# Four masked tiles to one crossbar transpose: a threshold attention with a two-layer block behind it

## The chip, the cores and the metric

The kernel runs on one core of a Trainium2 chip. The metric is the device time of one execution in microseconds (us). Before the change three timed runs gave 505.51, 511.03 and 508.68 us; the median is 508.68.

The names used below are those of the profile. PE is the matrix engine, PEld its loading of weights. DVE, ACT and POOL are the vector, scalar and general engines, and SP is an engine that only issues DMAs here. "SPq" and "ACTq" are the queues of SP and ACT, where DMAs are issued.

## The reference: what is computed

For 8 batches and 8 heads, with 576 rows of 64 elements, the attention keeps only the scores that come within tau = 0.02 of their row's largest one. The result, put together as 4608 rows of 512, goes through a block of two layers (512 to 2048 to 512) whose nonlinearity is h - tanh(h).

```python
scores = scale * np.matmul(q, k.transpose(0, 1, 3, 2))
thresh = np.max(scores, axis=-1, keepdims=True) - tau
scores = np.where(scores >= thresh, scores, -1000000000.0)
attn = np.exp(scores - np.max(scores, axis=-1, keepdims=True))
attn = attn / (np.sum(attn, axis=-1, keepdims=True) + 1e-09)
x = np.matmul(attn, v)            # then (batch, row, head * 64)
h = x @ w_in
out = (h - np.tanh(h)) @ w_out
```

## The kernel before

**Tiles.** Two heads make a pair; there are 32 pairs. A pair has 1152 query rows, which are nine tiles of 128 rows, so there are 288 tiles, numbered i. Each tile has 576 scores per row. Even tiles are of kind A and odd ones of kind B, and an A with the B behind it is a couple: most of the work on weights is done by couples.

**One tile's way.** `scores(i)` (L387) lets PE make the scores from the halves of q and k, of which k is there in a second form with its halves swapped (kS); DVE copies them out of the accumulator, scaled, into a buffer `sc` and finds the row's maximum (L420). `shift(i)` (L426) makes the bias tau minus maximum for a couple on DVE (L432). `kink(i)` (L439) is the mask: one ACT instruction (L447) turns each score below the threshold into a huge negative number and writes a half of the couple's buffer `z`, 128 x 576 in bf16. Then z has to be transposed, in nine blocks of 128 columns for a couple. In the first six pairs (54 tiles, `on_pe`, L57) PE does so (L466) and ACT takes the exponential from its accumulator (L475). From pair 6 on a crossbar transpose does it, a DMA that SP issues once for each couple (L454), 117 in all; its result is the buffer `zT`. `weights(i)` (L456) lets ACT take the exponential of the nine blocks in one instruction (L483, result `pT`), and `attend(i)` (L488) multiplies them with v on PE (L506, L513, L524). `norm` divides by the sum on DVE, and `emit_x` (L551) transposes the result on PE into the input of the layers.

**Other transposes.** From pair 8 or 9 on, q and k are also transposed by the crossbar (L315, 24 and 23 transposes), from the same SP queue. SP also issues the loads of the weights (L739, L743), the loads of q, k and v of the first pairs, and the stores of the output (L620, L626). Later loads of q, k and v are issued by ACT (L175).

**Layers.** The two layers work on blocks of 512 rows, made by four pairs. For each block there are 16 hidden steps, h (`hidden`, L575: four matmuls, L579; then tanh on ACT, L592, and a product on DVE, L598), and 16 projection steps, y (`project`, L603: four matmuls each, L605). They are spread over the slots of the attention by hand, as strings: one sign for a slot, h or y for a step.

**Order.** The program is written out by hand, and each engine takes its instructions in that order. The loop at L852 runs over slots s from -8 on. In slot s stand: the scores of tile s + AHEAD (8 slots ahead of the tile's own slot), the masks of tile s + MASK (5 ahead), the tanh of hidden steps written in an earlier slot, the weights of the tile whose turn it is, the layer steps of the slot, DVE's product, and the attention of the tile LAG = 2 slots behind its weights. `SOONER` (L844) takes the weights of the first four pairs four slots ahead. The loads, splits and transposes of q, k and v stand in a table of distances to the pair's first scores (L747 to L817), so they move with AHEAD.

**Buffers.** A buffer of a pool is given out again in turn, and its next writer waits until its last reader is done: for z in the crossbar part the reader is the transpose, which is done when it has landed. `z` has 4 buffers of two tiles each, `zT` 6, `sc` AHEAD - MASK + 2 = 5. So a couple's first mask waits for the transpose of the couple four before.

The lines around the change:

Of the kernel before, what the change touches and what calls it, by code (L numbers as in the profile page):

```python
# [10 lines left out]
BF16 = mybir.dt.bfloat16  # L11
# [3 lines left out]
ACT = mybir.ActivationFunctionType  # L15
# [3 lines left out]
def kernel(  # L19
# [11 lines left out]
    nc = tc.nc  # L31
    P = 128

    B, H, S, D = q.shape
# [9 lines left out]
    STEEP = 1.0e30  # L44

    HPAIR = H // 2
# [5 lines left out]
    TPP = 9  # L52
    NTILE = NPAIR * TPP
# [3 lines left out]
    def on_pe(i):  # L57
        p, j = divmod(i, TPP)
        return p < 6

    W = 2 * S

    AHEAD = 8
    LDK = 16
    MASK = 5
    LAG = 2


# [30 lines left out]
    for i in range(6):  # L99
# [8 lines left out]
    pool = lambda name, bufs, **kw: ctx.enter_context(  # L108
        tc.tile_pool(name=name, bufs=bufs, **kw)
    )  # L110
# [3 lines left out]
    qk_pool = pool("qk", 3)  # L114
    sc_pool = pool("sc", AHEAD - MASK + 2)
    st_pool = pool("st", 12)
    z_pool = pool("z", 4)
    zt_pool = pool("zt", 6)
    p_pool = pool("p", 3)
    o_pool = pool("o", 2)  # L120
    wt_pool = pool("wt", 4)
# [177 lines left out]
    def k_lead(p):  # L299
        if p < HPAIR + 2:  # L300
            return 6 if p in (2, 4) or p == HPAIR + 1 else 5 - (p == 1)
        return (6, 6)[1 - p % 2]

    def q_by_dma(p):

        return p >= DUAL
# [33 lines left out]
    def turn_first(t, part):  # L340

        hl = hls[0, t[0]]
        c0, c1 = ((0, 5), (5, TPP))[part]
        pl, tag = (ps_y, "y") if t == "ks" else (ps_h, "h")
        ps = pl.tile([P, 5 * P], FP16, name=f"ps1_{t}", tag=tag)
        for c in range(c0, c1):
            o = ps[:, (c - c0) * P : (c - c0 + 1) * P]
            if t == "ks":
                for a in range(2):
                    turn_chunk(o[64 * a : 64 * a + 64, :], c, hl[:, c, 1 - a, :])  # L350
            else:
                turn_chunk(o, c, hl[:, c, :, :].rearrange("p a d -> p (a d)"))
        if part == 0:
            mats[0, t] = qk_tile(t)
        dst, n = mats[0, t][:, c0 * P : c1 * P], (c1 - c0) * P
        if part == 1 or t == "q":
            nc.scalar.copy(out=dst, in_=ps[:, 0:n])
        else:
            nc.vector.tensor_copy(out=dst, in_=ps[:, 0:n])
# [15 lines left out]
    scs, mxs, nbs, zs, zts, pts, ops = {}, {}, {}, {}, {}, {}, {}  # L375

    def kind(i):

        return "AB"[i % 2]

    def place(i):

        p, j = divmod(i, TPP)
        j = j - p % 2
        return (p, None, 4) if j in (-1, 8) else (p, j // 4, j % 4)
# [40 lines left out]
    def shift(i):  # L426

        if kind(i) == "A":
            return
        mx = mxs.pop(i)  # L430
        nb = st_pool.tile([P, 9], F32, name="nb", tag="nb")
        nc.vector.tensor_scalar(  # L432
            out=nb.rearrange("p (a b) -> p a b", b=3)[:, :, 0:2],
            in0=mx.rearrange("p (a b) -> p a b", b=4)[:, :, 0:3],
            scalar1=-1.0, scalar2=tau, op0=ALU.mult, op1=ALU.add,
        )
        nbs[i - 1], nbs[i] = nb[:, 0:1], nb[:, 1:2]

    def kink(i):  # L439
        sc, nb = scs.pop(i), nbs.pop(i)  # L440
        if kind(i) == "B":
            zt = zs.pop(i - 1)
            z = zt[:, S:W]
        else:
            zt = zs[i] = z_pool.tile([P, W], BF16, name="z")
            z = zt[:, 0:S]
        nc.scalar.activation(  # L447
            out=z, in_=sc, func=ACT.Prelu, bias=nb, scale=1.0, alpha=STEEP
        )
        if on_pe(i):  # L450
            zts[i] = zt
        elif kind(i) == "B":
            zts[i] = zt_pool.tile([P, TPP, P], BF16, name="zT")
            nc.sync.dma_start_transpose(out=zts[i], in_=zt)  # L454

    def weights(i):  # L456

# [130 lines left out]
    def bend():  # L588
        while halves:
            m, n, ps = halves.pop(0)  # L590
            th = t_pool.tile([P, MB], F32, name="th", tag="th")
            nc.scalar.activation(out=th, in_=ps, func=ACT.Tanh)  # L592
            ths.append((m, n, ps, th))

    def shrink():
        while ths:
            m, n, ps, th = ths.pop(0)
            nc.vector.scalar_tensor_tensor(  # L598
                out=gs[m][:, n, :], in0=th, scalar=-1.0, in1=ps,
                op0=ALU.mult, op1=ALU.add,  # L600
            )

    def project(m, ms, part, ps, last, cols=slice(0, d_model)):  # L603
# [26 lines left out]
                    )  # L630


    EARLY = lambda m: 3 if m else 3
    LAST = 1

    PATTERN = lambda m: {
        0: '-h--h-hh--h-hh-h-hh-h--hh-h--hh-y-yy',
        B - 2: 'hyhyhyhyhyhyhyhyhyhyhyhyhyhyhyhy',
    }.get(m, 'h-yhyhhyhyyhyyhh-yhhyhhy-yhyyh-yyhhy')

# [3 lines left out]
    def layers(m, tail, pattern=None):  # L644
# [27 lines left out]

        now = quarters(m - 1)[EARLY(m - 1) :] if m > 0 else []
        if m < NMB - 1:
            now += quarters(m)[: EARLY(m)]
        else:
# [3 lines left out]

        ahead = n - max(0, EARLY(m) - 3) - LAST if m < NMB - 1 else n - 9 - LAST
        steps, at, i = [], [], 0
# [46 lines left out]
    def w_cast():  # L729
        flat, wt, i, cols = loaded.pop(0)  # L730
        nc.gpsimd.tensor_copy(out=flat[:, i * cols : (i + 1) * cols], in_=wt)
# [52 lines left out]
    for p in range(DUAL, NPAIR):  # L784
        first = TPP * p - AHEAD
        at = lambda d, f: plan.setdefault(first - d, []).append(f)
# [11 lines left out]
    for p in range(1, DUAL):  # L798
        first = TPP * p - AHEAD
        for d, f in PREP[3 if p == 1 else 0 :]:  # L800
            d -= p == 1 and d == 3
            if p > HPAIR and d >= LDK - 2:
                d = ((16, 14, 12), (17, 15, 13))[1 - p % 2][LDK - d]
            elif d in (7, 8) and q_by_dma(p):
                d = ((9, 9) if d == 7 else (10, 10))[1 - p % 2]
            elif p in LEADS and d in (8, 7, 5, 4):
                d = LEADS[p][(8, 7, 5, 4).index(d)]
            elif d == 4:
                d = 4
            elif d == 5:  # L810
                d = k_lead(p)
            elif p in (2, 4):
                d = {8: 9, 7: 8}.get(d, d)
            plan.setdefault(first - d, []).append(lambda p=p, f=f: f(p))
        d = (6, 7)[1 - p % 2] if q_by_dma(p) else 3 - (p == 1 or p >= 5)
        d = LEADS[p][4] if p in LEADS else d
# [21 lines left out]
    for at in sorted(plan):  # L838
        if at < -AHEAD:
            plan.setdefault(-AHEAD, []).extend(plan.pop(at))  # L840

    SOONER = (4, 4, 4, 4, 0, 0, 0)  # L844
    kinks, wts, atts = {}, {}, {}
    for i in range(NTILE + 3):
        at = i - SOONER[min(i // TPP, 6)]
        atts.setdefault(at + LAG, []).append(i)
        if i < NTILE:
            wts.setdefault(at, []).append(i)  # L850
            kinks.setdefault(i // 2 * 2 + 2 - AHEAD if i < 4 else i - MASK, []).append(i)
    for s in range(-AHEAD, NTILE + LAG + 3):  # L852
        p, j = divmod(max(s, 0), TPP)
        if 0 <= s < NTILE and j == 2 + LAG and p % HPAIR == 0 and p >= HPAIR:
            assert not todo
            todo = [(s + i, step) for i, step in layers(stage, False, PATTERN(stage))]
            stage += 1
        if s == NTILE:
            todo = [(s + n, step) for n, step in enumerate(layers(stage, True))]
            stage += 1  # L860
        if 0 <= s + AHEAD - 1 < NTILE:
            shift(s + AHEAD - 1)

        n = s + AHEAD
        if 0 < n < NTILE and place(n)[1] is None and kind(n) == "B":
            scores(n - 1)
        if 0 <= n < NTILE and (place(n)[1] is not None or kind(n) == "B"):
            scores(n)
        if s == 1 - AHEAD:
            for t in ("k", "q", "ks"):  # L870
                turn_first(t, 1)
        for i in kinks.pop(s, []):
            kink(i)
        bend()
        for i in wts.pop(s, []):
            weights(i)
        while todo and todo[0][0] <= s < NTILE + FIRST:
            todo.pop(0)[1]()
        if s == 0:
            nc.vector.tensor_tensor(  # L880
                out=fold, in0=ident_bf[:, 0:64], in1=ident_bf[:, 64:P], op=ALU.add
            )
        shrink()
        for store in going:
            store()
        going = stores[:-1]
        del stores[:-1]
        for i in atts.pop(s, []):
            pp, jj = divmod(i, TPP)
            if i < NTILE:  # L890
                attend(i)
                odd = pp % 2
                if jj == 3 + odd:
                    norm(pp, 0)
                elif odd and jj in (0, 8):
                    norm(pp - (jj == 0), 1)
            if pp and jj == 1 + pp % 2:
                emit_x(pp - 1)
        for step in plan.pop(s, []):
            step()  # L900
        for _ in range(cast_when.count(s + AHEAD)):
            w_cast()
        for _ in range(load_when.count(s + AHEAD)):
            w_load(next(pieces))
# [56 lines left out]
```

## Time and profile before

| | |
|---|---|
| timed runs, us | 505.51, 511.03, 508.68 (median 508.68) |
| span of the profiled execution, us | 509.7 |
| mean granted clock of PE | 0.997 |
| PE busy, us | 484.8 |
| ACT busy, us | 431.7 |
| DVE busy, us | 400.2 |
| POOL busy, us | 291.4 |
| mask L447 on ACT | 288 x 770 ns |
| exponential L483 on ACT | 117 x 1155 ns |
| tanh L592 on ACT | 128 x 583 ns |
| transposes zT on SP | 117, issue 1.47 us in the median |
| the same, from issue to landing, us | 3.2 least, 4.7 median, 9.8 most |

The span reaches from the first to the last instruction of one execution, which the hardware profiler recorded. An engine's busy time is the time in which its instructions were in work; overlapping instructions count once. Issuing a DMA and waiting count as no work. Matmuls are pipelined and their ends are modelled, so a busy PE need not be one at its peak. An idle time is put down to the event that ended it, for instance "ACT pT L483 <- DMA zT<-z": ACT's instruction in line 483 began when a transpose had landed.

### The profile page before, as it was taken

Reading aid. Unit: us, or ns where it says so; the run is one execution under the profiler, and the core shown is the slowest. Engines: PE = TensorE matmul, PEld = TensorE weight load, DVE = VectorE, ACT = ScalarE, POOL = GpSimd, SP = SyncE. Lnnn points to the kernel's source line nnn. Section 1 sums busy time; section 2 is a strip of 40 time slices with the busy share of each in tenths; the row PEclk is TensorE's granted clock in tenths of the full one; section 3 lists DMA queues with packets and bytes.
Section 4 is the critical chain, followed back from the end, with each engine's and each line's share of the span. In section 5 each row is a group of like instructions: output and inputs, shape, how many; then the busy total and the mean of one; then the engine's idle time right before and its main releaser. Section 6 shows DMA issues by size and latency. Waiting matters only on the chain.

```text
span 509.7 us, 12184 instructions
## 1 busy us (share of the span) xinstructions
PE 484.8 (95%) x4283; PEld 270.9 (53%) x4345; DVE 400.2 (79%) x1150; ACT 431.7 (85%) x617; POOL 291.4 (57%) x390
## 2 busy tenths in 40 slices
PE   8999899889999989999999999999998999999997
PEld 4666566445555545555555555555554555544444
DVE  5899978878889879988898789889886887544440
ACT  5999998889999889999999999899979999533430
POOL 8999999886765375757675666569456700000000
PEclk9999999989999999999999999999999999999999
DMA  7852658999999999999999999999999986311013
GB/s 206 262 155 89 195 190 220 159 225 214 231 217 245 192 254 209 238 241 242 242 195 221 261 238 225 207 242 240 213 191 258 187 144 115 87 41 42 23 41 82
DMA packets 233341, 95.32 MB, mean 187 GB/s; under 512 B 203968, under 2 KB 222656, under 8 KB 233280
## 3 DMA queue, kind: packets, MB, share of 16 engines
q1 hardware_dynamic: 212336, 72.87, 75.1%
q10 hardware_dynamic: 20944, 21.67, 16.1%
q8 instruction: 34, 0.56, 0.5%
q14 instruction: 27, 0.22, 0.2%
HBM read 36.70 MB, written 9.44 MB: 91 GB/s over the span
## 4 chain that ended last, share of the span: by engine, by line
PE 57%; POOL 12%; DMA 9%; issue 7%; ACT 7%; DVE 5%; ACTq 1%; SPq 0%; POOLq 0%; DVEq 0%
PE psY L605 18%; PE psH L579 14%; PE psS L410 13%; DMA zT<-z 6%; PE psO L513 3%; POOL kS L337 3%; PE psHt L579 3%; ACT pT L483 3%; DMA vraw<-in_v_dram 3%; ACT z L447 2%; DVE g L598 2%; POOL qhl L232 2%; DVE sc L420 2%; PE psS L401 2%; ACTq L175 1%
## 5 line engine op out<-in xcount | busy, mean ns | idle before, releaser
L420 DVE TENSOR_SCALAR_CACHE_REDUCE sc<-psS 128x576 f32<-128x576 f32 x288 | 213.5, 752 | 27.1 <-PE psS L410 12.9
L447 ACT ACTIVATE z<-sc,nb 128x576 bf16<-128x576 f32 x288 | 216.1, 770 | 8.0 <-DVE nb L432 5.7
L483 ACT ACTIVATE pT<-zT 128x1152 f16<-128x1152 bf16 x117 | 135.2, 1155 | 12.3 <-DMA zT<-z 10.6
L605 PE MATMUL psY<-w_out_sb,g 128*128 128x512 bf16 (+1 forms) x564 | 140.8, 373 | 1.6 <-issue 0.2
L579 PE MATMUL psH<-xT,w_in_sb 128*128 128x512 bf16 x448 | 119.4, 381 | 5.1 <-issue 2.0
L337 POOL COPY kS<-kT 64x1152 f16<-64x1152 f16 x62 | 70.8, 1142 | 86.3 <-DMA kT<-khl 72.7
L598 DVE SCALAR_TENSOR_TENSOR g<-th,psH 128x512 bf16<-128x512 f32 x128 | 87.6, 685 | 33.6 <-ACT th L592 32.9
L410 PE MATMUL psS<-kT,qT 128*128 128x512 f16 (+1 forms) x512 | 104.7, 286 | 4.1 <-DVE sc L420 1.9
L410 PE MATMUL psS<-kS,qT 128*128 128x512 f16 (+1 forms) x512 | 105.1, 287 | 0.0
L410 PEld LDWEIGHTS <-qT 128*128 128x128 f16 x1024 | 72.5, 98 | 59.0 <-issue 3.8
L592 ACT ACTIVATE th<-psH 128x512 f32<-128x512 f32 x128 | 74.6, 583 | 21.4 <-PE psH L579 21.4
L605 PEld LDWEIGHTS <-g 128*128 128x128 bf16 x592 | 51.1, 98 | 54.6 <-DVE g L598 0.4
L579 PEld LDWEIGHTS <-w_in_sb 128*128 128x128 bf16 x576 | 49.4, 98 | 57.4 <-issue 6.3
L513 PE MATMUL psO<-vb,pT 128*128 128x65 bf16 x1024 | 53.3, 194 | 0.0
L513 PEld LDWEIGHTS <-pT 128*128 128x128 f16 x1024 | 44.2, 98 | 9.6
L232 POOL TENSOR_TENSOR qhl<-qraw,qhl 128x576 f16<-128x576 f32 x31 | 39.7, 1281 | 2.6
L232 POOL TENSOR_TENSOR khl<-kraw,khl 128x576 f16<-128x576 f32 x31 | 39.7, 1280 | 2.7
L475 ACT ACTIVATE pT<-psZ 128x512 f16<-128x512 bf16 (+1 forms) x54 | 35.1, 654 | 2.4 <-PE psZ L466 2.1
L506 PE MATMUL psO<-vb,pT 128*128 128x130 bf16 x128 | 28.2, 220 | 3.7 <-ACT pT L483 3.6
L617 DVE COPY yo<-psY 128x512 f32<-128x512 f32 (+1 forms) x31 | 21.1, 680 | 13.1 <-PE psY L605 12.4
L539 DVE TENSOR_TENSOR osb<-psO,rc 128x256 bf16<-128x256 f32 x64 | 27.2, 424 | 2.2
L228 POOL TENSOR_SCALAR qraw<-qraw 128x576 f32<-128x576 f32 x31 | 20.8, 671 | 11.1 <-DMA qraw<-in_q_dram 10.8
(77 smaller groups left out, 452.1 us busy)
## 6 DMA issues: line engine op xcount, KB each, us to landing
out_dram<-yo SPq DMA_DIRECT2D x32, 256.0 KB, 3.8
kraw<-in_k_dram ACTq DMA_DIRECT2D x24, 288.0 KB, 4.2
qraw<-in_q_dram ACTq DMA_DIRECT2D x24, 256.0 KB, 4.3
wt<-in_moe_w_in_dram SPq DMA_DIRECT2D x8, 512.0 KB, 4.6
wt<-in_moe_w_out_dram SPq DMA_DIRECT2D x8, 512.0 KB, 3.9
vraw<-in_v_dram ACTq DMA_DIRECT2D x24, 160.0 KB, 4.3
vraw<-in_v_dram ACTq DMA_DIRECT2D x24, 128.0 KB, 3.8
vraw<-in_v_dram SPq DMA_DIRECT2D x8, 256.0 KB, 3.6
```

Of the source, the lines that this page charges most:

```text
L232: nc.gpsimd.tensor_tensor(out=hl[:, :, 1, :], in0=x, in1=hl[:, :, 0, :], op=ALU.subtract)
L337: nc.gpsimd.tensor_copy(out=o, in_=i)
L410: nc.tensor.matmul(out=ps[:, dst], lhsT=lhs, rhs=cols(p, kk, hh), start=(n == 0), stop=(n == 1),)
L420: nc.vector.tensor_scalar(out=sc, in0=ps[:, lo : lo + S], scalar1=SC, scalar2=None, op0=ALU.mult, op1=ALU.max, accum_out=mx[:, c : c + 1],)
L447: nc.scalar.activation(out=z, in_=sc, func=ACT.Prelu, bias=nb, scale=1.0, alpha=STEEP)
L475: nc.scalar.activation(out=pt[:, off * P : (off + n) * P], in_=ps[:, 0 : n * P], func=ACT.Exp)
L483: nc.scalar.activation(out=pt[:, 0 : n * P], in_=zts.pop(i)[:, 0:n, :], func=ACT.Exp)
L513: nc.tensor.matmul(out=po[:, t - 1 + ab, :], lhsT=pt[:, blk * P : (blk + 1) * P], rhs=vb[:, hh, c, :], start=False, stop=(n == 7), skip_gr ...
L579: nc.tensor.matmul(out=ps, lhsT=w_in_sb[:, c, n * P : (n + 1) * P], rhs=xs[m][:, c, :] if m < B else xR[:, c, :, :], start=(c == 0), stop= ...
L592: nc.scalar.activation(out=th, in_=ps, func=ACT.Tanh)
L598: nc.vector.scalar_tensor_tensor(out=gs[m][:, n, :], in0=th, scalar=-1.0, in1=ps, op0=ALU.mult, op1=ALU.add,)
L605: nc.tensor.matmul(out=ps, lhsT=gs[m][:, n, ms * P : (ms + 1) * P], rhs=w_out_sb[:, n, cols], start=(n == 0), stop=(n == DF_C - 1),)
```

## The change

Two couples, that is four tiles, now share one z buffer of 2304 columns and one zT buffer of 18 blocks; together they are called a quad. The masks of all four write their quarter of it, and SP issues one transpose of 18 blocks behind the fourth mask. In the crossbar part 117 transposes become 59: 58 of 18 blocks and, for the last couple, one of 9. In the part that PE transposes, the quad's buffer is only shared, and PE turns each tile as before. z has 2 buffers in place of 4 and zT 3 in place of 6, each of twice the size. So the first mask of a quad waits for the transpose of the quad before the last.

Masks stand seven slots ahead in place of five, and scores ten in place of eight; the loop begins two slots earlier. The weights of the first four pairs stand six slots ahead and those of pairs 4 and 5 four (before: four and none). The first block of layers begins in slot 36 (before 40) and lasts 40 slots, with five projection steps of its own (before three); the second block has two projection steps fewer. The later blocks keep their slots and their patterns. No instruction of PE, DVE, ACT or POOL is added or removed.

```diff
--- before.py
+++ after.py
@@ -60,9 +60,9 @@
 
     W = 2 * S
 
-    AHEAD = 8
+    AHEAD = 10
     LDK = 16
-    MASK = 5
+    MASK = 7
     LAG = 2
 
 
@@ -114,8 +114,8 @@
     qk_pool = pool("qk", 3)
     sc_pool = pool("sc", AHEAD - MASK + 2)
     st_pool = pool("st", 12)
-    z_pool = pool("z", 4)
-    zt_pool = pool("zt", 6)
+    z_pool = pool("z", 2)
+    zt_pool = pool("zt", 3)
     p_pool = pool("p", 3)
     o_pool = pool("o", 2)
     wt_pool = pool("wt", 4)
@@ -436,22 +436,32 @@
         )
         nbs[i - 1], nbs[i] = nb[:, 0:1], nb[:, 1:2]
 
+    FIRST_DUO = sum(on_pe(i) for i in range(NTILE)) // 2
+    LAST_DUO = NTILE // 2 - 1
+    quads = {}
+
     def kink(i):
         sc, nb = scs.pop(i), nbs.pop(i)
-        if kind(i) == "B":
-            zt = zs.pop(i - 1)
-            z = zt[:, S:W]
-        else:
-            zt = zs[i] = z_pool.tile([P, W], BF16, name="z")
-            z = zt[:, 0:S]
+        d = i // 2
+        late = (d if on_pe(i) else d - FIRST_DUO) % 2
+        if kind(i) == "A" and not late:
+            quads[0] = z_pool.tile([P, 2 * W], BF16, name="z")
+        z4 = quads[0]
+        zt = z4[:, late * W : (late + 1) * W]
+        c = int(kind(i) == "B")
         nc.scalar.activation(
-            out=z, in_=sc, func=ACT.Prelu, bias=nb, scale=1.0, alpha=STEEP
+            out=zt[:, c * S : (c + 1) * S], in_=sc, func=ACT.Prelu, bias=nb,
+            scale=1.0, alpha=STEEP,
         )
         if on_pe(i):
             zts[i] = zt
-        elif kind(i) == "B":
-            zts[i] = zt_pool.tile([P, TPP, P], BF16, name="zT")
-            nc.sync.dma_start_transpose(out=zts[i], in_=zt)
+        elif kind(i) == "B" and (late or d == LAST_DUO):
+            n = TPP * (1 + late)
+            t4 = zt_pool.tile([P, 2 * TPP, P], BF16, name="zT")
+            nc.sync.dma_start_transpose(out=t4[:, 0:n, :], in_=z4[:, 0 : n * P])
+            if late:
+                zts[i - 2] = t4[:, 0:TPP, :]
+            zts[i] = t4[:, late * TPP : (late + 1) * TPP, :]
 
     def weights(i):
 
@@ -630,11 +640,12 @@
                     )
 
 
-    EARLY = lambda m: 3 if m else 3
+    EARLY = lambda m: 3 if m else 5
     LAST = 1
 
     PATTERN = lambda m: {
-        0: '-h--h-hh--h-hh-h-hh-h--hh-h--hh-y-yy',
+        0: '-h--h-hh--h-hh-h-hh-h--hh-h--hh--yy-yy-y',
+        1: 'h-yhyhhyhy-hyyhh-yhhyhhy-yhy-h-yyhhy',
         B - 2: 'hyhyhyhyhyhyhyhyhyhyhyhyhyhyhyhy',
     }.get(m, 'h-yhyhhyhyyhyyhh-yhhyhhy-yhyyh-yyhhy')
 
@@ -841,7 +852,7 @@
 
 
 
-    SOONER = (4, 4, 4, 4, 0, 0, 0)
+    SOONER = (6, 6, 6, 6, 4, 4, 0)
     kinks, wts, atts = {}, {}, {}
     for i in range(NTILE + 3):
         at = i - SOONER[min(i // TPP, 6)]
@@ -851,7 +862,7 @@
             kinks.setdefault(i // 2 * 2 + 2 - AHEAD if i < 4 else i - MASK, []).append(i)
     for s in range(-AHEAD, NTILE + LAG + 3):
         p, j = divmod(max(s, 0), TPP)
-        if 0 <= s < NTILE and j == 2 + LAG and p % HPAIR == 0 and p >= HPAIR:
+        if 0 <= s < NTILE and j == (2 + LAG if p > HPAIR else 0) and p % HPAIR == 0 and p >= HPAIR:
             assert not todo
             todo = [(s + i, step) for i, step in layers(stage, False, PATTERN(stage))]
             stage += 1
```

## The prediction

> **What bounds the kernel now.** The page's first and second parts come first: which engine is full, and where.
>
> ```profile
> PE 484.8 (95%) x4283; PEld 270.9 (53%) x4345; DVE 400.2 (79%) x1150; ACT 431.7 (85%) x617; POOL 291.4 (57%) x390
> ...
> PE   8999899889999989999999999999998999999997
> ACT  5999998889999889999999999899979999533430
> ```
>
> PE is busy for 95% of the span and ACT for 85%, but ACT's row falls only behind slice 34, where the attention has ended; before that both stand at nines. The table of stretches puts numbers on it. Its columns are the stretch in us, its length, and the busy time (instructions) of PE, weight loads, DVE, ACT and POOL, then clock, DMA share and GB/s.
>
> ```profile
> 75.00:116.00 41.00, 35.85 (x353) 21.34 (x357) 33.48 (x100) 36.15 (x54) 35.28 (x44) 0.96 1.07 207
> 116.00:200.00 84.00, 81.34 (x717) 44.26 (x729) 71.78 (x213) 80.39 (x110) 53.52 (x68) 1.00 1.19 221
> 200.00:300.00 100.00, 98.76 (x873) 54.44 (x887) 88.53 (x263) 96.31 (x133) 63.72 (x82) 1.00 1.18 236
> 300.00:400.00 100.00, 96.25 (x851) 52.68 (x865) 85.52 (x254) 93.59 (x128) 63.70 (x82) 1.00 1.22 223
> ```
>
> From 116 to 400 us PE is busy 276.4 of 284 us and ACT 270.3: both are nearly full, and the DMA share is above 1 (packet times overlap). So nothing in this change can win much there, because it removes no instruction of PE, DVE or ACT; but it can lose much, since a stall of ACT has little reserve to be made up from. Only 75 to 116 us, where the crossbar transposes begin, holds 5 us of idle PE.
>
> Third, the list of waits (total us, times, longest) and the source view of the transposes.
>
> ```profile
> ACT pT L483 <- DMA zT<-z: 10.6, 11, 2.2
> ...
> PE psO L506 <- ACT pT L483: 3.6, 4, 1.3
> ```
>
> ```profile
> L454 SPq DMA_TRANSPOSE zT<-z x117: 1242/1470/3841, 81.3 to 433.4; - x117
> ...
> DMA to landing us min/median/max: 3.2/4.7/9.8
> ```
>
> A transpose takes SP 1.24 us to issue at least and 1.47 in the median, and lands 3.2 to 9.8 us after its issue began. ACT has waited for landings 11 times, 10.6 us in all, and of that 3.6 us came through to PE: a factor of 0.34. These numbers carry the sum below.
>
> **The change, part by part.**
>
> *Transposes.* 117 of 9 blocks become 58 of 18 and a last one of 9. Blocks and bytes stay, so SP's issue work stays about the same (117 x 1.47 = 172 us) unless an issue has a large fixed part. I count nothing for it: SP is on no chain.
>
> *How long 18 blocks take.* The trace shows none. Seen from the issue of the last mask's transpose, the nine added blocks cost nothing if they only fill a queue in which the first transpose stood anyway, and might gain 0.5 us if half as many completions thin the queue. At the other end they cost twice the least issue time, 2.5 us, if descriptors and data of the added blocks add up. I take one least issue time, 1.24 us: in the undisturbed transpose at 414.93 us the data ran from 1.17 to 2.7 us behind the start of an issue of 1.28 us, so issue and data overlap and one issue time is what nine more blocks add.
>
> *The Trainium skill* speaks for the change here. "DMA: Bandwidth & Descriptors", section "Anatomy of one DMA — SWDGE (gpsimd) path", gives a DMA issued by GpSimd about 2.0 us plus its bytes over 436 GB/s; for 294,912 bytes that is an estimate of 2.7 us, twice 5.4, and 3.4 for one of double size. Where this row of fixed costs occupied the queue, each quad would win 2.0 us of it. But the trace has transposes whose data follow one another without a gap when both are queued (228.7 us), so the fixed part is latency beside other transfers, and I leave it out.
>
> *Masks seven ahead.* The last mask of a quad now runs seven slots ahead of its own weights, and the first couple's exponential comes five slots behind that mask, as before. So its time to land is the same, and the transfer is longer. The second couple has seven slots.
>
> *z in two buffers of four.* This is the new wait. The first mask of a quad writes the buffer that the quad before the last has left, so it waits for that transpose to land. Between the last mask of that quad and this one lie four masks: five slots, where before it was seven. In the trace one such distance looks like this (start, duration, line).
>
> ```profile
> 200.47 0.77 ACT L447 ACTIVATE z<-sc,nb 128x576 bf16<-128x576 f32 x1
> 201.13 0.58 ACT L592 ACTIVATE th<-psH 128x512 f32<-128x512 f32 x1
> 201.61 0.77 ACT L447 ACTIVATE z<-sc,nb 128x576 bf16<-128x576 f32 x1
> ...
> 202.28 1.16 ACT L483 ACTIVATE pT<-zT 128x1152 f16<-128x1152 bf16 x1
> 203.33 1.45 ACT L447 ACTIVATE z<-sc,nb 128x576 bf16<-128x576 f32 x2
> ...
> 206.21 0.76 ACT L447 ACTIVATE z<-sc,nb 128x576 bf16<-128x576 f32 x1
> 206.88 0.58 ACT L592 ACTIVATE th<-psH 128x512 f32<-128x512 f32 x1
> ...
> 207.35 0.77 ACT L447 ACTIVATE z<-sc,nb 128x576 bf16<-128x576 f32 x1
> ```
>
> The mask that ends at 201.24 is transposed by an issue at 202.63 that lands at 206.28; the mask at 207.35 would have to wait for it. Time given 6.1 us, used 5.0, left 1.1. Taken so for every second transpose of the trace (57 places), the time given has a median of 6.1 us and the landing one of 5.3; in 21 places the landing is already the later one. A wait also gives the next quad as much time, for that one's transpose is issued before it. Going through the 57 in order with this credit, the waits add up to 11 us with landings 0.5 us sooner, 18 unchanged, 37 with 1.24 us more, 66 with 2.5 us more.
>
> Behind the waiting mask stand, in ACT's order, the tanh of the hidden layer (DVE's product and then the projection wait for it), the exponential (attention two slots on) and the loads of q, k and v that ACT issues. I take 37 us. The exponential's 10.6 us go, because it comes later in the slot than the mask that waits for the same landing. Of the added 26.3 us a share of 0.34 reaches PE: **+9 us**.
>
> *Stages moved.* The first layer block starts at slot 36 and scores ten ahead, so 46 slots behind the first score and not 48. Evictions of scores run from 7.8 us (first) to 65.2 (the 49th), 1.2 us a slot, and the first hidden matmul starts at 67.0. PE gets layer work 2.4 us sooner, and of that it loses the two slots of attention, about 1.9 us less 0.5: I count **-1 us**. Five projection steps for three in block 0 and two fewer in block 1 only move work. The exponentials of pairs 4 and 5 come four slots sooner, which leaves a four-slot pause where the transposes begin, and the first transpose moves from slot 58 behind the first score to 60, away from the last weight loads. In the trace that start was jammed: transposes issued at 87.9 and 91.3 us took 9.8 and 9.5 us, and PE stood idle 1.27, 0.77 and 1.55 us before matmuls at 98.9, 102.0 and 104.0. The gain lies between nothing and these 3.6 us; I take **-2**.
>
> *Queued behind a transpose.* kT, qT and stores wait in SP's queue up to 1.24 us longer. qT had 1.6 us or more to spare in pairs 9 to 31, kS 2.6: nothing, as long as that holds; beyond it PE waits with each pair.
>
> The rest (pools of equal bytes, sc still five buffers, kT and qT turned at the same distance from their scores) costs nothing; PE's own work hides it, as it is the same.
>
> **Sum.** 509.7 + 9 - 1 - 2 = 515.7 us against the profiled span. The median of the runs, 508.7, lies 1.0 below it: 514.7, so **515**. (The page knows nothing of that execution beyond its span.)
>
> **Rivals.** *Faster, 501:* the eighteen blocks land within the 6.1 us that ACT has, because half as many transfers leave shorter queues. Then the waits for landings go (10.6 x 0.34 = 3.6 us), the jam goes (3.6) and the early block gives 1: 508.7 - 8.2 = 500.5. It decides where the landing's median stays below about 5 us with few over 6. For it speaks that transposes of 9 landed in 3.2 us when alone; against it that 21 of 57 overshoot already.
>
> *Same, 509:* landings stay as they are behind the second transpose. (18 - 10.6) x 0.34 = +2.5, less 3.
>
> *Much slower, 525 to 532:* with 2.5 us more, (66 - 10.6) x 0.34 = +19, less 3: 524.7; or with 37 us, but all of the added 26.3 reaching the end, less 3: 532. ACT's fullness speaks for it; against it that ACT still had 14 us idle from 116 to 400.
>
> *Not what it says:* if the buffer were free earlier than the landing, no mask would wait. The written order has a DMA wait on the first mask of each quad, so I give this no share.
>
> **Numbers.** Forecast 0.46 (its own range 511 to 521, a fifth of it below 513.8), much slower 0.16, faster 0.20, same 0.18. Within 1% of 508.7 is 503.6 to 513.8, about what three runs that spread from 505.5 to 511.0 can tell. Slower: 0.8 x 0.46 + 0.16 = 0.53; same: 0.18 + 0.09 = 0.27; faster 0.20. Range 502 to 527: it leaves out about half of each outer case.
>
> **What would show it.** Right: 59 transposes, issue near 2.6 us, landing median 5.5 to 6.5; in the list of waits a line of ACT z behind DMA zT with 25 to 45 us, next to none of pT behind zT; PE busy as before and its idle time in 116 to 400 us grown from 7.6 us by 8 or more; less idle before 116. Wrong: landings near 5 us, no such line on z, or a large one that leaves PE's idle time alone (the factor 0.34 is from eleven waits).

## The result: slower by 4.9%

The changed kernel takes 533.66 us in the median of four runs (532.28 to 535.09), the kernel before 508.94 beside it. The ratio is 1.0486, with a 95% interval of 1.042 to 1.0551. Its profiled execution has a span of 533.1 us, against 509.7 before.

The page of the changed kernel, engines and slices:

```profile
PE 493.8 (93%) x4345; PEld 272.8 (51%) x4345; DVE 399.0 (75%) x1150; ACT 431.5 (81%) x617; POOL 291.3 (55%) x390
...
PE   8999898888999889989898899889999999999997
ACT  5999987898989978888898888888998999643330
```

ACT does the same work, 431.5 us after 431.7, in a span that is 23.4 us longer. Its row now has eights where nines stood. (PE's busy time is no larger in truth: the trace of before lacks 62 of its matmul records, 4283 for 4345, and shows that much too little.) The table of stretches tells where the time went (columns as before):

```profile
75.00:116.00 41.00, 34.58 (x344) 20.22 (x342) 34.17 (x100) 35.05 (x53) 34.71 (x43) 1.00 0.89 204
116.00:200.00 84.00, 76.58 (x675) 41.20 (x674) 66.03 (x198) 73.84 (x101) 50.66 (x66) 1.00 1.12 209
200.00:300.00 100.00, 92.17 (x800) 49.43 (x798) 79.26 (x237) 86.04 (x118) 60.72 (x78) 1.00 1.11 208
300.00:400.00 100.00, 93.52 (x818) 50.59 (x817) 80.65 (x240) 89.62 (x123) 57.55 (x74) 1.00 1.10 215
```

Between 116 and 400 us ACT was busy 270.3 us before and is 249.5 now; PE went from 276.4 to 262.3. The clock stands at 1.00 in these four stretches. The list of waits names the event (total, times, longest):

```profile
DVE g L608 <- ACT th L602: 81.2, 88, 3.1
POOL kS L337 <- DMA kT<-khl: 70.2, 18, 7.6
ACT z L452 <- DMA zT<-z: 30.9, 21, 2.8
...
PE psH L589 <- DVE g L608: 8.6, 14, 1.4
PE psS L410 <- DVE sc L420: 8.0, 15, 1.4
```

The masks (L452) now wait for transposes, as forecast; no exponential does any more. Behind the masks the delay can be followed to PE: DVE waits 81.2 us for the tanh (45.4 before), and PE waits for DVE's products and for copied scores, 8.6 and 8.0 us (1.9 each before). The same lines of the kernel before:

```profile
DVE g L598 <- ACT th L592: 45.4, 55, 2.6
...
PE psS L410 <- DVE sc L420: 1.9, 7, 0.4
PE psH L579 <- DVE g L598: 1.9, 4, 0.9
```

One such wait, from the time lines of SP and of ACT (start, duration, line):

```profile
174.22 3.66 SPq L461 DMA_TRANSPOSE zT<-z  x1
```

```profile
176.29 1.46 ACT L452 ACTIVATE z<-sc,nb 128x576 bf16<-128x576 f32 x2
...
178.71 0.76 ACT L452 ACTIVATE z<-sc,nb 128x576 bf16<-128x576 f32 x1
...
180.84 0.78 ACT L452 ACTIVATE z<-sc,nb 128x576 bf16<-128x576 f32 x1 [0.89 <-DMA zT<-z]
181.52 0.58 ACT L602 ACTIVATE th<-psH 128x512 f32<-128x512 f32 x1
182.00 1.15 ACT L493 ACTIVATE pT<-zT 128x1152 f16<-128x1152 bf16 x1
```

The transpose issued at 174.22 landed at 180.73. The mask that reuses its buffer started 0.11 us later, after 0.89 us in which ACT did nothing, and the tanh and the exponential started late behind it. The exponential at 182.00 reads the same transpose and needs no wait of its own. The source view of the transposes, durations of the issue (least, median, most) and time to land:

```profile
L461 SPq DMA_TRANSPOSE zT<-z x59: 1278/3315/5554, 86.4 to 455.1; - x59
...
DMA to landing us min/median/max: 3.3/6.4/9.2
```

(The least values belong to the last transpose, of 9 blocks; of the 58 with 18 blocks the shortest issue took 2.28 us and the shortest landing 4.6.) Taken place by place in the trace, 33 of the masks that open a quad have an idle time ahead of them, 39.6 us in sum. 30 of these masks, with 37.8 us, started 0.1 us behind the landing that frees their buffer; the other three started over 1 us behind it, so that they waited for something else. The list has only 30.9 of it, since it puts a wait down to the semaphore that came last.

### The profile page after: what moved, and what is told of

The parts are those of the page before. It is cut to its first block, busy times and chain, and to the rows that moved or that the text cites. A ratio compares the mean times of both kernels' runs of the same rounds, so it can differ in the third digit from the quotient of the medians.

```text
span 533.1 us, 12010 instructions
## 1 busy us (share of the span) xinstructions
PE 493.8 (93%) x4345; PEld 272.8 (51%) x4345; DVE 399.0 (75%) x1150; ACT 431.5 (81%) x617; POOL 291.3 (55%) x390
## 4 chain that ended last, share of the span: by engine, by line
PE 23%; DMA 18%; ACT 7%; DVE 6%; POOL 4%; issue 3%; ACTq 1%; SPq 0%; POOLq 0%; DVEq 0%
DMA zT<-z 14%; PE psY L615 10%; PE psH L589 6%; ACT z L452 3%; DMA qraw<-in_q_dram 3%; PE psHt L589 3%; PE psS L410 2%; DVE sc L420 2%; ACT pT L493 2%; DVE g L608 2%; ACT th L602 2%; ACTq L175 1%; POOL kS L337 1%; DMA kT<-khl 1%; PE psO L523 1%
## 5 line engine op out<-in xcount | busy, mean ns | idle before, releaser
L452 ACT ACTIVATE z<-sc,nb 128x576 bf16<-128x576 f32 x288 | 217.1, 770 | 43.9 <-DMA zT<-z 30.9
L615 PE MATMUL psY<-w_out_sb,g 128*128 128x512 bf16 (+1 forms) x592 | 145.8, 374 | 0.0
L589 PE MATMUL psH<-xT,w_in_sb 128*128 128x512 bf16 x480 | 123.2, 379 | 8.7 <-DVE g L608 8.6
L410 PEld LDWEIGHTS <-qT 128*128 128x128 f16 x1024 | 73.9, 97 | 66.5 <-issue 11.3
L602 ACT ACTIVATE th<-psH 128x512 f32<-128x512 f32 x128 | 74.5, 582 | 21.2 <-PE psH L589 21.2
L228 POOL TENSOR_SCALAR qraw<-qraw 128x576 f32<-128x576 f32 x31 | 20.8, 671 | 25.2 <-DMA qraw<-in_q_dram 23.7
L627 DVE COPY yo<-psY 128x512 f32<-128x512 f32 (+1 forms) x31 | 21.0, 678 | 12.3 <-PE psY L615 12.0
```

Source lines behind the costliest of these rows:

```text
L410: nc.tensor.matmul(out=ps[:, dst], lhsT=lhs, rhs=cols(p, kk, hh), start=(n == 0), stop=(n == 1),)
L452: nc.scalar.activation(out=zt[:, c * S : (c + 1) * S], in_=sc, func=ACT.Prelu, bias=nb, scale=1.0, alpha=STEEP,)
L589: nc.tensor.matmul(out=ps, lhsT=w_in_sb[:, c, n * P : (n + 1) * P], rhs=xs[m][:, c, :] if m < B else xR[:, c, :, :], start=(c == 0), stop= ...
L615: nc.tensor.matmul(out=ps, lhsT=gs[m][:, n, ms * P : (ms + 1) * P], rhs=w_out_sb[:, n, cols], start=(n == 0), stop=(n == DF_C - 1),)
```

## The experiments

Each variant stands beside runs of the kernel before on the same chip, and the ratio is to those. Theory A: the wait for the z buffer is the loss. Theory B: the loss is the length of the transfer, whatever waits for it. Theory C: it lies in the moved slots.

### A third buffer for z

```diff
-    z_pool = pool("z", 2)
+    z_pool = pool("z", 3)
```

> The changed kernel with a third z buffer of four tiles; nothing else. If the loss is the wait of a quad's first mask for its buffer (theory A), that wait, 39.6 us in 33 places, falls to under 3 us, and what is left is the wait of the exponential for the same landing. The exponential starts 1.16 us behind the mask in the median; the landings of the changed kernel taken against that leave 13 us in 13 places. At 0.8 to 1.0 of the difference the time is 507 to 513 us. If the loss is the length of the transfer whatever waits for it (theory B), the wait only moves to the exponential, with 30 us or more, and the time stays above 524 us. If the loss lies in the slots of masks, scores and layers (theory C), the time stays near 533 us.

Measured: 523.19 us, ratio 1.0274 (1.0164 to 1.0384). The list of waits, of an execution that was the longest of four (span 527.4 us):

```profile
ACT pT L493 <- DMA zT<-z: 29.9, 22, 4.1
```

The masks wait no more for landings, but the exponentials do, 29.9 us, more than twice what was expected from the landings of the changed kernel. The estimate had used a time line that the masks' own waits had already stretched, the landings are a little longer here (6.6 us in the median), and the execution shown is the longest; that this is the whole difference is not shown. So theory A alone is too small, and B goes too far: 10.5 us came back. There are two distances of five slots in the changed kernel, to the next writer of z and to the exponential, and with the first one gone the second one binds.

### Short transposes, shared buffers

```diff
-        elif kind(i) == "B" and (late or d == LAST_DUO):
-            ...
+        elif kind(i) == "B":
+            zts[i] = zt_pool.tile([P, TPP, P], BF16, name="zT")
+            nc.sync.dma_start_transpose(out=zts[i], in_=zt)
```

> The changed kernel with a transpose of 9 blocks behind each couple, as before the change, but z still shared by four tiles in two buffers, and all slots of the changed kernel. Theory A with landings as before the change: 18 us of mask waits (the sum with credit at unchanged landings), so about 7 us more waiting than the 10.6 us before: 512 to 518 us. Theory B: the short transfer is back, so 506 to 511 us. Theory C: 525 us or more.

Measured: 529.42 us, ratio 1.0416 (1.0309 to 1.0523). The transposes are those of before again, 117 with a median landing of 4.6 us, and the masks wait:

```profile
ACT z L452 <- DMA zT<-z: 25.1, 15, 4.4
```

(zT has six buffers of one couple again.) Most of the loss is there without any transpose of 18 blocks. It takes only the buffers: two shared by four tiles give the awaited transpose five slots, where four of two tiles gave it seven. Theory A had the place right and its price too low. Both factors were short: 18 us of mask waits were expected and the list has 25.1, and more of them reached the end than the forecast's share allows.

### Couples in all, only the slots moved

This is the variant above with `z_pool` of 4 buffers of two tiles each.

> The changed kernel with transposes of 9 blocks and buffers of couples (four z, six zT), as before the change, so that only the slots differ: masks seven and scores ten ahead, weights of the first six pairs sooner, the first layer block in slot 36. Theories A and B: no wait of masks for landings, 506 to 511 us. Since the first exponential of the crossbar part came 4.5 us later in the changed kernel (93.9 against 89.4 us), theory C has a smaller form: 512 to 514 us. Theory C in full: 525 us or more.

Measured: 511.17 us (ten runs), ratio 1.0051 (1.001 to 1.0091). Theory C falls in its large form: the slots cost half a per cent, and by the interval no more than 0.9%. With seven slots from a couple's last mask to its exponential, and seven to the next writer of its buffer, only 2.1 us of waits for landings are left:

```profile
ACT z L451 <- DMA zT<-z: 2.1, 2, 1.9
```

This variant and the one above it differ in the z buffers alone: 511.17 against 529.42 us. These 18 us are the price of the shared buffers.

### Two slots more, with three buffers and with two

```diff
-    AHEAD = 10
+    AHEAD = 12
-    MASK = 7
+    MASK = 9
-    SOONER = (6, 6, 6, 6, 4, 4, 0)
+    SOONER = (8, 8, 8, 8, 6, 6, 0)
```

With three z buffers:

> The changed kernel with three z buffers and masks nine, scores twelve ahead (weights of the first six pairs two slots sooner too), so that a transpose of 18 blocks has seven slots to land before its first exponential. If the length of the transfer costs only through waits (theory A), those waits, 29.9 us with five slots, fall below 5 us, and the time is that of the variant with short transposes and the changed slots, 511 us, and up to 3 us more for two further slots at the start: 511 to 515 us. If 18 blocks in one cost by themselves, as by longer stays in the queue before the transposes of q and k (theory B), the time stays above 519 us.

Measured: 506.77 us (ten runs), ratio 0.9995 (0.9957 to 1.0034). No wait for a transpose is in the list. The transposes are as long as in the changed kernel (columns as above):

```profile
L461 SPq DMA_TRANSPOSE zT<-z x59: 1272/3361/4874, 84.9 to 423.3; - x59
...
DMA to landing us min/median/max: 3.2/6.4/8.8
```

So the same 59 transposes with the same landings cost nothing once both who wait for them, the next writer of z and the exponential, have seven slots or more. With the two z buffers of the changed kernel:

> The changed kernel with masks nine and scores twelve ahead, but with its two z buffers. Theory A, the buffer: the distance from a quad's last mask to the first mask of the quad after the next stays five slots, however far the masks lie ahead, so the waits of masks stay at 30 to 40 us and the time at 529 to 536 us. If it is the exponential's distance of five slots that counts (theory B), the time falls to that of the variant with three buffers, 505 to 510 us.

Measured: 533.65 us, ratio 1.0491 (1.0394 to 1.0587), as the changed kernel.

```profile
ACT z L452 <- DMA zT<-z: 25.6, 17, 3.5
```

Moving the masks further ahead is worth nothing while two buffers hold them. The two variants differ in one z buffer, and it decides over some 27 us.

### One slot more, three buffers

The same with AHEAD 11, MASK 8 and SOONER (7, 7, 7, 7, 5, 5, 0).

> The changed kernel with three z buffers, masks eight and scores eleven ahead: six slots from the last mask of a quad to its first exponential. With landings of 6.4 us in the median and six slots of 1.5 us less a mask and the exponential's place, few waits are left (under 8 us against 29.9 with five slots): theory A gives 505 to 511 us. If seven slots are needed, 512 to 518 us.

Measured: 514.94 us, ratio 1.0168 (1.0096 to 1.024).

```profile
ACT z L452 <- DMA zT<-z: 4.7, 4, 2.1
ACT pT L493 <- DMA zT<-z: 4.7, 3, 2.7
```

With six slots exponentials still wait, 4.7 us. The 4.7 us put down to masks are not the wait for the buffer: none of the four masks opens a quad, and each stands behind a load that ACT issues (L175) and that was held up. So the 1.7% is not the price of the six slots alone. By the intervals six slots differ from seven (0.9957 to 1.0034), but not from five (1.0164 to 1.0384).

### Couples with two slots more

Couples again, with the slots of the variant with two more (AHEAD 12, MASK 9, SOONER (8, 8, 8, 8, 6, 6, 0)).

> The slots of the variant with two more slots (masks nine, scores twelve ahead), but buffers and transposes of couples, 9 blocks each. If a transpose of 18 blocks gains nothing once its landing is covered: 505 to 509 us, as with three buffers of four (506.8). If fewer, longer transposes themselves spare the queue something: 510 to 513 us, as in the variant of couples with the changed slots (511.2).

Measured: 509.59 us (twelve runs), ratio 1.0025 (0.9982 to 1.0067). The interval overlaps that of the long transposes in the same slots (0.9957 to 1.0034), so that 58 fewer DMAs gain or cost anything by themselves is not shown. No variant beat the kernel before.

### What a delay of ACT costs

The step of the forecast that had no row of its own was the share of ACT's delay that reaches the end. The next four measure it. Theory D: ACT has no reserve but its few idle microseconds, wherever the delay lies. Theory P: the place decides, as tanh and products stand behind the mask. First an extra instruction in the kernel before, at the mask:

```diff
+            if not on_pe(i) and (i // 2) % 2:
+                nc.scalar.activation(
+                    out=spare, in_=sc, func=ACT.Prelu, bias=nb, scale=1.0, alpha=STEEP
+                )
```

> The kernel before the change with a second, unused mask instruction ahead of the first mask of every second couple in the crossbar part: 59 more ACT instructions of 0.67 us, 39.5 us in all, as much as the masks of the changed kernel waited, and at the same place in ACT's order. It measures what share of a delay of ACT reaches the end. With the predicted share of 0.34 the time is 509 + 13 = 522 us; if ACT has no reserve beyond its idle time of 14 us between 116 and 400 us, 509 + 25 = 534; if all reaches the end, 548 us.

Measured: 529.57 us, ratio 1.0418 (1.0345 to 1.0491): +20 us. The 59 instructions came cheaper than the 39.5 us expected: ACT's busy time grew by 35.7 us, to 467.4. Then the same ahead of the exponential (it reads the scores of the tile six further on):

> The kernel before the change with the extra, unused mask instruction ahead of the exponential of every second couple and not ahead of its mask: 57 of 0.67 us, 38 us. Theory D: as with the extra at the masks, 527 to 531 us. Theory P: less than half of it, 515 to 521 us.

Measured: 528.45 us, ratio 1.044 (1.038 to 1.05), for 33.2 us more of ACT's busy time. The table of stretches shows what both have in common; the fourth number after the stretch's length is ACT's. With the extra at the mask:

```profile
200.00:300.00 100.00, 95.40 (x832) 51.38 (x830) 81.78 (x244) 99.89 (x140) 58.18 (x75) 1.00 1.12 217
```

With the extra at the exponential:

```profile
200.00:300.00 100.00, 94.72 (x824) 51.22 (x837) 82.02 (x244) 100.00 (x141) 61.43 (x79) 1.00 1.16 223
```

ACT has next to no idle time left in either, and PE, which had 98.8 here before, is down to 95.4 and 94.7. Half the number, at the mask (`% 4 == 1`; it came to 29 instructions):

> The kernel before the change with the extra mask instruction ahead of the first mask of every fourth couple: 30 of 0.67 us, 20 us. The full number, 39.5 us, cost 20 us. Theory D, a reserve of ACT of about 20 us in all beyond which everything counts: 509 to 513 us. A constant share of one half: 519 us; the predicted share of 0.34: 516 us.

Measured: 515.25 us beside 507.52, ratio 1.0178 (1.0108 to 1.0248): 7.7 us for 16.4 us more of ACT's busy time. A sharp reserve of 20 us is out. In the profiled executions ACT's idle time from the 62nd to the 282nd mask falls from 18.7 us to 8.8 with half the number and to 3.4 with all of it, so the first half takes up more of it than the second. But by the intervals of the times (5 to 13 us for the half, 18 to 25 for all) a constant share of about one half is not excluded. Then the order within a slot, in the changed kernel:

```diff
-        for i in kinks.pop(s, []):
-            kink(i)
         bend()
+        for i in kinks.pop(s, []):
+            kink(i)
```

> The changed kernel with the tanh of a slot ahead of its masks and not behind them. If a wait of ACT costs by its place, since the tanh and the hidden layer's buffers stand behind the mask (theory P), the 40 us of waits cost only as much as the waits of the exponential did with three z buffers, 0.4 of them: 520 to 525 us. If ACT as a whole has no reserve left, wherever it waits (theory D), the time falls only by what the waits themselves lose, some 3 to 8 us for the later place in the slot: 526 to 531 us.

Measured: 528.92 us, ratio 1.0412 (1.0326 to 1.0497), with 26.0 us of waits of masks in the list. With the tanh ahead of the waiting mask most of the loss stays, as D has it and not P.

### Less work for ACT

```diff
-            nc.scalar.activation(out=th, in_=ps, func=ACT.Tanh)
+            nc.scalar.activation(out=th[:, 0 : MB // 2], in_=ps[:, 0 : MB // 2], func=ACT.Tanh)
```

(DVE's product, which then reads that half twice, is left out here.)

> The changed kernel with less work for ACT and nothing else moved: each tanh is taken of 256 of its 512 columns only, and DVE uses that half twice (so half of the hidden layer's result is left out). 256 columns are worth about 0.2 us, 128 times, some 20 us of it beside the crossbar transposes. If the waits come through because ACT has no reserve (theory D), this reserve takes them up: the time falls by 12 to 20 us, to 514 to 522 us, though the waits of masks stay at 25 to 40 us. If the waits reach PE by their place in the chain from mask to matmul, whatever ACT has to do (theory P), it stays above 527 us.

Measured: 524.89 us, ratio 1.0353 (1.0313 to 1.0393). The time lies between both expectations; the kernel before took 506.49 us beside it, and on the base of 508.94 the ratio would mean 527 us, at the edge of theory P. Of 27.3 us of tanh taken from ACT (74.5 to 47.2 us busy) only 7 (by the ratios) to 9 us (by the times) were won, because the waits grew:

```profile
ACT z L452 <- DMA zT<-z: 39.6, 30, 3.1
```

What lies between a quad's last mask and the mask that waits for its transpose is ACT's own work. Less of it means that ACT arrives sooner and waits longer. So a reserve of ACT does not simply take up such a wait, and theory D is not the whole account: the landing itself sets a pace.

## Why the prediction was wrong

The direction and the place of the waiting were right, and its amount came out near. The share of it that reaches the end was wrong, and with it the size: +6 us was forecast, and +24.7 came.

**The transposes.** 59, as said. The issue was put at 2.6 us and is 3.3 in the median; the landing was put at 5.5 to 6.5 us and has a median of 6.4. It was to be 1.24 us longer than before and is 1.7 longer (6.4 after 4.7).

**The waits.** 37 us were forecast on the masks and 37.8 are there behind landings, in the places named; the exponentials' 10.6 us are gone, as said. That the amount fits so well is in part luck. The same sum with the lengthening that came, 1.7 us, gives 46; and for short transposes in shared buffers it gave 18 where the list has 25. The working found the place, and the amount to within some ten microseconds.

**The share of 0.34: the step that failed.** The term "a share of 0.34 reaches PE: +9 us" came from 10.6 us of ACT's waits beside 3.6 us of PE's. It counted only PE's waits for the exponential itself; in the changed kernel PE's waits grew on two other paths, for DVE's products and for copied scores (8.6 and 8.0 us, 1.9 each before). And it came from eleven waits in a kernel with some idle time of ACT behind them. In the trace, the stretch from the 62nd mask to the 282nd is the same work for ACT in every variant with the full mask, tanh and exponential. Its length, with the idle time of ACT and of PE in it (the difference of the first two is ACT's work):

| kernel | stretch, us | ACT idle | PE idle |
|---|---|---|---|
| before | 333.4 | 18.7 | 12.3 |
| changed | 354.2 | 40.6 | 27.3 |
| short transposes, shared buffers | 345.7 | 32.5 | 20.4 |
| couples, slots moved | 331.5 | 16.8 | 8.7 |
| three buffers, two slots more | 324.3 | 12.8 | 8.2 |

ACT's work comes to 311 to 315 us in all of them, and the length follows its idle time: +20.8 us of length for +21.9 us idle. (PE's idle time in the first and the last row is a little too high, for the matmul records that these traces lack.) Before, the waits for landings were themselves in ACT's 18.7 us of idle: 10.6 us by the list, 12.3 place by place. Only 6 to 8 us were other idle time, and the 25 to 29 added microseconds of waiting could displace no more than these. In the changed kernel 40.4 of the 40.6 us idle stand ahead of masks. The forecast named "14 us idle from 116 to 400" as a reserve without taking the landing waits out of it.

So what the runs show in place of 0.34 is a share of 0.7 to 0.8 here: 20.8 us for 25 to 29 us of added waits. Variants with the same slots give 0.6 to 0.8, with the waits taken place by place: short transposes in shared buffers against couples 18.3 us for 23.7 us of waits (0.8), two z buffers against three with two slots more 26.9 for 34.8 (0.8), and the changed kernel against couples 22.5 for 35.6 (0.6). With extra work in place of waits it was about 0.5 to 0.6. Nothing shows a dependence on the place in the slot, and whether the share grows with the amount is not settled. Of work taken from ACT half comes back as waits (in this stretch 19 us less work and 9.4 us more idle time with the half tanh).

**The start: -1 and -2.** The first hidden matmul did start 3.0 us sooner (64.0 after 67.0), and the first transposes landed in 6.2, 7.0 and 6.5 us where two of before took 9.8 and 9.5. Neither won time: PE's busy time in the first 116 us is 103.4 us after 103.7, so the work done sooner took other work's place. And couples with only the slots moved took 0.5% longer than the kernel before, not less.

**Queued transposes of q and k.** No wait of PE for qT stands among the list's larger lines, so the "nothing" put down for them held.

**The rivals.** "Much slower", with all of the added waits reaching the end, gave 532 us and had 0.16. It comes nearest, in part by luck: a share of 1 is too high, which makes up for a gain of 3 us that did not come and for the half per cent that the slots cost. The first rival (landings short enough) fails on its own point: the median is 6.4 us and not below 5.

**The fixed cost per DMA.** Leaving it out agrees with the runs: with the landing covered, 59 transposes and 117 differ by less than the intervals (506.77 and 509.59 us).

## What to carry to other kernels

Halving the number of buffers while doubling each kept the bytes and lost time here, because the awaited transpose had five slots in place of seven. So count, in slots, from the last write of a group to the first write that reuses its buffer, and compare that with the landing before thinking of the transfer's size. Moving the producers further ahead helped only the consumer at the end of the chain and not the writer of the buffer: that one needed a third buffer.

Where two engines are nearly full, take the waits in question out of an engine's idle time before calling the rest a reserve. A share read off a few small waits on one path did not hold for more than three times as much on others.

## What the runs showed of the hardware

A crossbar transpose of twice the blocks does not take twice as long to land: 6.4 us in the median after 4.7, while its issue on SP takes 3.3 after 1.5, more than double (the shortest, 2.28 after 1.24, a little under). In the variant with three buffers and two slots more the medians are the same, 6.4 and 3.4, so they do not come from the waits.

The instruction queue's packets of 16 KB (34 in each of these executions, one about every 14 us, 0.9 to 2.0 us each) coincide with stalls of transposes: in the kernel before, about 20 packets of 256 B took over 0.7 us each around 90, 107, 123, 137, 164 and 180 us, where such a packet began at 90.8, 105.9, 121.8, 136.0, 164.2 and 179.5, and the usual packet takes 18 ns. The four longest landings (8.4 to 9.8 us) all had such a packet in flight. Two groups of slow packets, at 96.5 and 99.7 us, have none near. No run tried to move them, so that they are the cause is not shown.
